# Attention with negated scores: one pass that clips and finds the least, 1/sum by way of HBM, and a new written order

## The chip, the cores and the metric

The kernel runs on one core of one Trainium2 chip. Its time is device time in microseconds (us) of one execution; the figure used is the median of several runs. The engines of a core are TensorE (PE; its weight loads are PEld), VectorE (DVE), ScalarE (ACT), GpSimd (POOL) and SyncE (SP), which here issues every DMA.

## The reference, cut

```python
q_bits = (np.einsum('bhsd,dk->bhsk', q, proj) > 0).astype(np.int64)
k_bits = (np.einsum('bhsd,dk->bhsk', k, proj) > 0).astype(np.int64)
powers = 2 ** np.arange(n_bits)
q_bucket = np.sum(q_bits * powers, axis=-1)
k_bucket = np.sum(k_bits * powers, axis=-1)
mask = q_bucket[:, :, :, None] == k_bucket[:, :, None, :]
scores = scale * np.matmul(q, k.transpose(0, 1, 3, 2))
scores = np.where(mask, scores, -1000000000.0)
scores = scores - np.max(scores, axis=-1, keepdims=True)
attn = np.exp(scores)
attn = attn / (np.sum(attn, axis=-1, keepdims=True) + 1e-09)
return np.matmul(attn, v).astype(np.float32)
...
h = x @ w_in
r = np.maximum(h, 0.0)
g = s * (r * r) + b
return (g @ w_out).astype(np.float32)
...
a = x @ w1
b = x @ w2
h = a * b @ w3
return (h @ w_out).astype(np.float32)
```

The first part is attention over 2 batches of 8 heads, 768 rows, head dimension 64, scale 1/8, with a mask from 6 hash bits. Its output, as 1536 tokens of 512, goes through the second part (512 to 2048 and back) and then the third (two projections to 1024, their product, two more matrices). All of it is float32.

## The kernel before

**Tiling.** Attention runs head by head (16 heads), each in 3 units of 256 query rows, and a unit in two halves of 128 rows (`unit`). For a half, four matmuls write one score tile `sc`, 128 x 768, in PSUM: two of q and k, and two that add products of hash bits, by which every differing bit lowers a score by 2^100 (`mask`, with `thr` and `sgn`). Four operand tiles of a head (`q1`, `q2`, `k1`, `k2`) hold high and low parts of q and k and the mask rows; for head 0 engines build them by halves (`begin`), for the others six DMAs of 64 x 768 per head move their rows (`move`, L373, on SP). The score tiles have two buffers, so a third score waits until `exp` has read the first.

**From score to exp.** Four steps per half, 96 halves in all: DVE takes the row's maximum, negated (`negm`, L487); DVE makes `gate`, which is 1/8 where the row has any unmasked score and 0 else (L495); DVE makes `bias` = negm x gate (L502); ACT computes `p` = exp(sc x gate + bias) and the row's sum `ssum` (L510).

**From exp to output.** PE transposes `p` in 128 x 128 blocks into `t` (L524, 12 to a unit, four to a PSUM tile). Each `t` is split in a high and a low part: two of three by ACT and DVE (L562, L566), the third by ACT and POOL (L545, L550 or L552, L556). PE multiplies them with v into `o` (L530, L531). ACT and DVE add the halves of `o` into `xf` (L579, L583), where two heads stand together.

**1/sum** (`norm`, once for each pair of heads and unit, 24 times): DVE takes the reciprocal of four sums per row (`r`, L604), POOL spreads it to 128 x 256 (`rb`, L610), PE transposes it in two blocks into a PSUM tile `rt` (L620), and DVE multiplies `xf` with it (L624). Then `xf` becomes high and low parts of x (`put_x`).

**The rest.** The second part (`layer1`) multiplies weights with x, three matmuls per product of high and low parts (`h`, `x` at L705); its batch 0 runs between the attention of batch 1. The third part (`layer2`) follows (`psw`, `p`, `y`). Weights come as float64 halves and are taken apart on DVE, ACT and POOL (`convert`, L255 to L269) during attention, are kept in HBM and fetched again.

**Order.** Nothing is scheduled at run time. `Plan` collects the operations; `ORDER` is a table that gives the order in which they are emitted, `WAYS` picks an engine where an operation has several, and `PLACES` gives each tile its buffer. Each engine and the one DMA queue of SP work their instructions off in that order, each waiting for its semaphores. 24 matmuls on a tile of ones (`warm`, L308) stand in the first 26 us on PE, six ahead of the first real ones, the others between the first scores.

Of the kernel before, what the change touches and what calls it, by code (L numbers as in the profile page):

```python
# [38 lines left out]
NW2 = 14  # L39
POOL = {(b, u, 1) for b in range(2) for u in range(3)}  # L40
# [8 lines left out]
    "CqEgFdDNDgDECrDkDODIEhDFCsEkEiDlDJDBEjElFeCwDpDPDhDGDvEmCxE4EnDqDiEoDKE5EQDmEUDLDwDrE9DnEVE6DMDQE7DjE+E8HFDo"
    "EZE/ERDRHMFha6EaHNHGFAESDsFBHLEbEtCyEpFiDtEWIeHHFfFjNdDuDxFmEuFkEXHIFlETFnHJDSEqEyCzHKHODUGBFoDTHPFpErDyFqEY"  # L50
    "DzEcGCFCEvEdGGEzGDEeEwFGGEE0GFHQEsGHHEFLD0FDaoExDVGIFHGjD1GJFEGKE1FIGkFrF6E2FJFvFMGlGoGmE3GnFNFFIgGpFKFwF0Ga"
    "FsInIhF7HTGqGbGrImF1FtFOGsHUGLFxGPKQFPF2HYaxFgGQHVHWFQIkHXHZG8IfIiFyFuIlIpHsGMHaIjF8HRGUHbHtIqFzHSHcagF3GNIo"
    "GtGRGVHuHxHvF4GWGSHwG2HyGxIFGyF5IrHzH0GOayH1IGF9GzGTGXF+GuIHIKF/IIGYGvG0G3HdGZIJHhG4GwKSILG1HeG5GAKaHiIMHfHm"
    "LsG6GcIuINKTKZG9HnG7KYGdIOIvHgH2HoIzG+H3IwGeKUHjIxH4H/IyHkI0H6IsJOH7I1KVItHlGfI2JPG/I3KWGhHpHAKbIAJHJQKXJTGi"
    "LrHqH8JRIBIYKcJSITH9JUIPHBJwHrIUHCJVJWH5JIKdJxJXGgH+KRICazIQI8IVJyIDJ1IRI9IWJzIEI4IZJ2ISJ0JBLtJ3IXIaI5KgLuL0"
    "J4JCI6LzJ5IbKhL1JcJYIcJDJJKlJdI+KiKjIdLxKkI/KmLvI7KeLyL2K5KfJZKnLwa0JhKoK6L3JnJAKpawJEJeJaaYJ+JiK7JfJ6K8JFL4"
    "JjK+K9O4JGKDa1JbJ/K/Jga2J7LSKJKAJoa3LAKKLBJ8JkLCLTJKKuJlJpLXJLKEKBLUJmKvKqLVKFJMJ9LWLYNfKCKGKrLZNgNmKzLaKHNl"
    "KsL7L5bJKILbJqL8KtJNLDK0L9MAJrL+K1JuL/LHKwMBNhKLLIKxMbNiLELMMCLFNjL6MDMcKMMEKyNoK2NnKNLNMdNkMgLJK3MeMULcLOJs"
# [1151 lines left out]
```

## Time and profile before

| | us |
|---|---|
| median of 3 runs | 761.66 (759.51 to 762.94) |
| profiled execution, own time | 762.2 |
| profiled execution, span | 760.4 |

| engine | busy us | share of the span | instructions |
|---|---|---|---|
| PE | 743.4 | 98% | 4392 |
| DVE | 611.4 | 80% | 1221 |
| ACT | 394.3 | 52% | 763 |
| POOL | 286.1 | 38% | 328 |

The busy time of an engine is the union of its instructions from start to end. Matmuls overlap on PE, so a PE that is busy all the time may still start its matmuls later than it could; what a matmul costs in a dense stretch is the distance between two starts, not its duration. Shares are means over the span: attention with little else fills PE's queue up to about 150 us, attention and the second part together up to about 370 us, then come matrices alone.

### The profile page before, as it was taken

To read this page: it belongs to the slowest core of one execution; us is meant where nothing else is said; L and a number is where in the kernel's file an instruction comes from. 1 tells how busy PE (TensorE), PEld (TensorE's weight loads), DVE (VectorE), ACT (ScalarE), POOL (GpSimd) and SP (SyncE) were. 2 spreads that over 40 slices of the span, in tenths; PEclk is the share of its full clock that TensorE was granted. 3 is DMA by queue.
4 is the path that set the end of the run, shared out by engine and by line. 5 is a ranking of instruction groups with operands and counts; after the bars stand their busy time and mean duration, and the time that the engine had idled before them with its cause. 6 is when DMAs were issued, how large, how long until landed. Compare 5 with 4: busy or idle time off the path is not lost.

```text
span 760.4 us, 12708 instructions
## 1 busy us (share of the span) xinstructions
PE 743.4 (98%) x4392; PEld 700.7 (92%) x4392; DVE 611.4 (80%) x1221; ACT 394.3 (52%) x763; POOL 286.1 (38%) x328
## 2 busy tenths in 40 slices
PE   8899999999999999999999999999999999999998
PEld 6898999899998999999999998999998999899996
DVE  7999999999999999998999676775889966655442
ACT  5888898888656666747454242243443321221002
POOL 2577788884635654535311131123304300001101
PEclk9999999999999999999999999999999999999999
DMA  7556565356267674365697997778899997474712
GB/s 223 156 127 175 166 191 145 103 140 198 73 176 234 203 228 144 94 222 174 242 330 238 306 326 250 240 246 286 288 334 346 332 324 254 153 253 130 230 33 84
DMA packets 73823, 159.63 MB, mean 210 GB/s; under 512 B 7328, under 2 KB 41504, under 8 KB 73760
## 3 DMA queue, kind: packets, MB, share of 16 engines
q1 hardware_dynamic: 73760, 158.82, 65.6%
q8 instruction: 35, 0.57, 0.3%
q14 instruction: 28, 0.23, 0.1%
HBM read 99.94 MB, written 41.16 MB: 186 GB/s over the span
## 4 chain that ended last, share of the span: by engine, by line
PE 81%; DVE 11%; DMA 3%; ACT 2%; issue 1%; POOL 0%; POOLq 0%; ACTq 0%; DVEq 0%; SPq 0%
PE x L705 15%; PE h L705 14%; PE p L705 14%; PE y L1149 9%; PE sc L473 7%; PE t L524 6%; PE psw L1108 5%; PE o L530 3%; PE o L531 3%; DVE negm L487 2%; PE bits L445 2%; DVE pt L566 1%; ACT p L510 1%; DMA raw_wo<-in_wo 1%; DMA raw_w_a<-in_w 1%
## 5 line engine op out<-in xcount | busy, mean ns | idle before, releaser
L705 PE MATMUL h<-x,w_wi 128*128 128x384 f32 x768 | 149.8, 339 | 1.8 <-DVE rl L779 1.4
L705 PE MATMUL x<-g,w_wo 128*128 128x384 f32 x768 | 146.5, 337 | 0.8 <-DMA w_wo<-kept_wo 0.5
L705 PEld LDWEIGHTS h<-x,w_wi 128*128 128x128 f32 x768 | 132.7, 188 | 5.9 <-DVE rl L779 2.5
L705 PEld LDWEIGHTS x<-g,w_wo 128*128 128x128 f32 x768 | 133.4, 188 | 3.3 <-issue 0.8
L510 ACT ACTIVATE p<-sc,bias,gate 128x768 f32<-128x768 f32 x96 | 95.7, 997 | 25.6 <-DVE bias L502 19.8
L1078 DVE TENSOR_TENSOR c<-c,p 128x384 f32<-128x384 f32 x112 | 60.3, 552 | 58.5 <-PE p L705 53.2
L487 DVE TENSOR_REDUCE negm<-sc 128x1 f32<-128x768 f32 x96 | 90.9, 949 | 6.4 <-PE sc L473 5.5
L473 PE MATMUL sc<-k,q 128*128 128x384 f32 x384 | 88.8, 354 | 1.8 <-ACT p L510 1.8
L524 PE MATMUL t<-ident,p 128*128 128x128 f32 x576 | 84.0, 275 | 3.5 <-DVE pt L566 1.3
L530 PE MATMUL o<-pt,vv 128*128 128x256 f32 x288 | 78.5, 299 | 0.3 <-DVE xf L583 0.2
L705 PE MATMUL p<-x,w 128*128 128x384 f32 x384 | 76.5, 336 | 0.6 <-DVE c L1078 0.6
L524 PEld LDWEIGHTS t<-ident,p 128*128 128x128 f32 x576 | 67.6, 141 | 9.0 <-DVE pt L566 2.3
L531 PE MATMUL o<-pt,vv 128*128 128x256 f32 x288 | 73.4, 282 | 0.1
L556 POOL TENSOR_TENSOR pt<-pf,pt 128x512 fp32r<-128x512 f32 x48 | 63.2, 1316 | 26.9 <-ACT pt L552 22.8
L705 PEld LDWEIGHTS p<-x,w 128*128 128x128 f32 x384 | 67.9, 188 | 4.0 <-DVE c L1078 1.2
L473 PEld LDWEIGHTS sc<-k,q 128*128 128x128 f32 x384 | 66.3, 194 | 3.7 <-ACT p L510 3.1
L566 DVE TENSOR_TENSOR pt<-t,pt 128x512 fp32r<-128x512 f32 x96 | 65.1, 681 | 4.2 <-ACT pt L562 3.5
L562 ACT CAST pt<-t 128x512 fp32r<-128x512 f32 x96 | 55.7, 586 | 20.0 <-PE t L524 13.7
L530 PEld LDWEIGHTS o<-pt,vv 128*128 128x128 f32 x288 | 54.3, 189 | 2.6 <-DVE xf L583 1.6
L531 PEld LDWEIGHTS o<-pt,vv 128*128 128x128 f32 x288 | 54.5, 189 | 0.4 <-DVE gate L495 0.3
L784 ACT ACTIVATE g<-rl,b_bc 128x384 fp32r<-128x384 f32 x64 | 39.0, 614 | 24.4 <-DVE rl L779 12.6
L1108 PE MATMUL psw<-w_wo,w_w 128*128 128x512 f32 x192 | 51.3, 394 | 0.0
(257 smaller groups left out, 1291.9 us busy)
## 6 DMA issues: line engine op xcount, KB each, us to landing
w<-kept_s SPq DMA_DIRECT2D x64, 256.0 KB, 5.4
...
```

The costliest lines, as they stand in the source:

```text
L473: nc.tensor.matmul(sc()[:, i, :HALF], x[:, t], y[:, i * HALF : (i + 1) * HALF], start=st, stop=not st)
L487: lambda j=j, sc=sc: nc.vector.tensor_reduce(negm()[:, j : j + 1], sc()[:, :, :HALF], AX.XY, ALU.max, negate=True),
L510: lambda j=j, k=k, sc=sc: nc.scalar.activation(ps[j](), sc()[:, :, :HALF], AF.Exp, bias=bias()[:, j : j + 1], scale=gate()[:, j : j + 1], ...
L524: nc.tensor.transpose(tp()[:, e, j * P : (j + 1) * P], flat[:, c * P : (c + 1) * P], ident)
L530: nc.tensor.matmul(o()[:, :U], w, pt()[:, 0, e], start=(c == 0), stop=False)
L531: nc.tensor.matmul(o()[:, :U], w, pt()[:, 1, e], start=False, stop=(c == NC - 1))
L556: lambda pf=pf, pt=pt: nc.gpsimd.tensor_tensor(pt()[:, 1], pf(), r32(pt()[:, 0]), ALU.subtract),
L566: lambda tp=tp, pt=pt: nc.vector.tensor_tensor(pt()[:, 1], tp(), r32(pt()[:, 0]), ALU.subtract),
L705: nc.tensor.matmul(ps()[:, :n], x, y, start=(i == 0 and e == 0), stop=(i == len(terms) - 1 and e == 2))
L1078: "cadd", "dve", 0.47, rank, lambda: nc.vector.tensor_tensor(x(out), a(), p(), op), [(ps, 1), *reads], writes
L1108: nc.tensor.matmul(ps(), w3()[:, p, c], wo()[:, q], start=(j == 0 and e == 0), stop=(j == 7 and e == 2))
L1149: nc.tensor.matmul(y(), abt()[:, p, c], wt()[:, q], start=(i == 0 and e == 0), stop=(i == DF2 // P - 1 and e == 2))
```

## The change

Scores come out negated. q is multiplied with -1/8 as it is loaded (a new operation of 64 x 768 per head, L380 of the new file; for head 0 the factor `qs` goes into the split), the projection gets a factor that undoes this for the bits, and the signs of the mask are turned, so that a differing bit raises a score by 2^100. One DVE instruction per half then clips the score tile at 10^9, in place in PSUM, and finds the row's least value with its accumulator (`least`, L513). exp takes that as bias and -1 as scale (L521). `gate` and `bias` are gone. A fully masked row is all 10^9 and gives exp(0) everywhere, as the reference asks.

1/sum: DVE writes each reciprocal eight times into 128 x 32 (L617) and transposes that in 32 x 32 blocks (L624); two DMAs write rows of 32 into HBM (`rd`, L630), two DMAs read them back, spread over 64 partitions each (`rb`, L640); DVE or POOL multiplies (L644). `rt` and its two transposes on PE are gone, and the spreading on POOL.

Of the warm-up matmuls 15 remain, in one row ahead of all else (`warm`, L312). The tables `ORDER`, `WAYS` and `PLACES` are new as a whole.

```diff
...
+OUT = 1e9
...
+NWARM = 15
...
-    "AgAAAEAhAaCEAVaZAUCFABAiACAXAjADaRAkAZAoahAnAtAKApAuAlAyAxAGCGAmAvAqAYAwA0CNATAzCMCHAbAsD2AHA1ArCIA2CSaaA+CJ"
+    "XyAkA6XjBpAxXkAsXzAyAoBtXqAtA3A7DMApBuX0DNA4A8AqA5BPBvXlBsX1AuBMEbXmXrArBQAvAzBRDOAwBNA0XnDVBBA1DUByXsA2DPX5"
...
+    qs = const.tile([P, 1], F32, name="qs")
+    nc.vector.memset(qs[:D], -(D**-0.5))
+    nc.vector.memset(qs[D:], 1.0)
...
-    for a, t, f in ((0, 2.0**-126, 1.0), (32, 0.0, -1.0), (64, 0.0, -BIG), (96, 2.0**-126, BIG)):
+    for a, t, f in ((0, 2.0**-126, -1.0), (32, 0.0, 1.0), (64, 0.0, -BIG), (96, 2.0**-126, BIG)):
...
-        plan.op(
-            "neg_p", "dve", 0.1, LATER, lambda: nc.vector.tensor_scalar_mul(pj[:, 32:96], pj[:, 32:96], -1.0),
-            [("pj", 0)], [("pj", 1)],
-        )
+        def signs():
+
+            a, c = pj.rearrange("p (a n) -> p a n", n=D)[:, :, : D // 2], pj[:, :D]
+            nc.vector.tensor_scalar_mul(a, a, -1.0)
+            nc.vector.tensor_scalar_mul(c, c, D**0.5)
+
+        plan.op("neg_p", "dve", 0.2, LATER, signs, [("pj", 0)], [("pj", 1)])
...
-        for i in range(24):
-            tw = plan.tile(ps_o, 1, [P, 512], F32, "o", f"warm_{i}", 2)
-            plan.op(
-                "warm", "pe", 0.12, LATER,
-                lambda tw=tw: nc.tensor.matmul(
-                    tw()[:, :U], ones()[:, 0, 0, :P], ones()[:, 0, 0], start=True, stop=True
-                ),
-                [(ones, 0)], [(tw, 0)],
-            )
+        tw = plan.tile(ps_o, 1, [P, 512], F32, "o", "warm", 2)
+
+        def warm_up():
+            for _ in range(NWARM):
+                nc.tensor.matmul(tw()[:, :U], ones()[:, 0, 0, :P], ones()[:, 0, 0], start=True, stop=True)
+
+        plan.op("warm", "pe", 0.12 * NWARM, LATER, warm_up, [(ones, 0)], [(tw, 0)])
...
-                copy(f"split_h{ph}", (0.73, 0.8), q1, t, [(t, 0)], [(q1, 0)])
-                rest(f"split_l{ph}", 1.8, k2, t, q1, [(t, 0), (q1, 0)], [(k2, 0)])
+                less = lambda eng: eng.tensor_scalar(t()[:D], t()[:D], -(D**-0.5), 1.0, ALU.mult, ALU.mult)
+                plan.op(
+                    f"scale{ph}", "pool", 0.8, LATER, lambda: less(nc.gpsimd), [(t, 0)], [(t, 1)],
+                    (
+                        ("dve", 0.46, lambda: less(nc.vector)),
+                        ("act", 0.85, lambda: nc.scalar.mul(t()[:D], t()[:D], -(D**-0.5))),
+                    ),
+                )
+                copy(f"split_h{ph}", (0.73, 0.8), q1, t, [(t, 1)], [(q1, 0)])
+                rest(f"split_l{ph}", 1.8, k2, t, q1, [(t, 1), (q1, 0)], [(k2, 0)])
...
-                ways(f"split_h_0{i}", lambda c=c: q1()[:, c], lambda c=c: t()[:, c], [(t, i)], [(q1, 0, i)])
+                times = lambda eng, c=c: eng.tensor_scalar(q1()[:, c], t()[:, c], qs, 1.0, ALU.mult, ALU.mult)
+                plan.op(
+                    f"split_h_0{i}", "act", 0.52, -500,
+                    lambda c=c: nc.scalar.activation(q1()[:, c], t()[:, c], AF.Copy, scale=qs), [(t, i)], [(q1, 0, i)],
+                    (("dve", 0.43, lambda f=times: f(nc.vector)), ("pool", 0.75, lambda f=times: f(nc.gpsimd))),
+                )
...
-                    lambda c=c: nc.vector.tensor_tensor(k2()[:, c], t()[:, c], r32(q1()[:, c]), ALU.subtract),
+                    lambda c=c: nc.vector.scalar_tensor_tensor(
+                        k2()[:, c], t()[:, c], qs, r32(q1()[:, c]), ALU.mult, ALU.subtract
+                    ),
...
-            negm, gate, bias = (plan.tile(sm_p, 4, [P, NQ], F32, t, f"{t}_{m}") for t in ("negm", "gate", "bias"))
+            least = plan.tile(sm_p, 4, [P, NQ], F32, "least", f"least_{m}")
...
-                    f"max{j}{ph}", "dve", 0.87, LATER,
-                    lambda j=j, sc=sc: nc.vector.tensor_reduce(
-                        negm()[:, j : j + 1], sc()[:, :, :HALF], AX.XY, ALU.max, negate=True
+                    f"max{j}{ph}", "dve", 1.03, LATER,
+                    lambda j=j, sc=sc: nc.vector.tensor_scalar(
+                        sc()[:, :, :HALF], sc()[:, :, :HALF], OUT, None, ALU.min, ALU.min, accum_out=least()[:, j : j + 1]
...
-                    [(sc, 0)], [(negm, j)],
-                )
-
-                plan.op(
-                    f"gate{j}{ph}", "dve", 0.07, LATER,
-                    lambda j=j: nc.vector.tensor_scalar(
-                        gate()[:, j : j + 1], negm()[:, j : j + 1], BIG / 1024, D**-0.5, ALU.is_lt, ALU.mult
-                    ),
-                    [(negm, j)], [(gate, j)],
-                )
-                plan.op(
-                    f"bias{j}{ph}", "dve", 0.13, LATER,
-                    lambda j=j: nc.vector.tensor_scalar_mul(
-                        bias()[:, j : j + 1], negm()[:, j : j + 1], gate()[:, j : j + 1]
-                    ),
-                    [(gate, j)], [(bias, j)],
+                    [(sc, 0)], [(sc, 1), (least, j)],
...
-                        ps[j](), sc()[:, :, :HALF], AF.Exp, bias=bias()[:, j : j + 1], scale=gate()[:, j : j + 1],
+                        ps[j](), sc()[:, :, :HALF], AF.Exp, bias=least()[:, j : j + 1], scale=-1.0,
...
-                    [(sc, 0), (gate, j), (bias, j)], [(ps[j], 0), (ssum, (h % 2, k))],
+                    [(sc, 1), (least, j)], [(ps[j], 0), (ssum, (h % 2, k))],
...
-            plan.op(
-                f"r{b}", "dve", 0.08, at_, lambda: nc.vector.reciprocal(r()[:, :, c], ssum()[:, :, c]),
-                [(ssum, ("e", u))], [(r, u)],
-            )
-            rb = plan.tile(sm_p, 1, [P, NQ, 2, D], F32, "rb", f"rb_{m}")
-            plan.op(
-                f"rb{b}", "pool", 0.35, at_,
-                lambda: nc.gpsimd.tensor_scalar(
-                    rb(), r()[:, :, c].rearrange("p a k -> p k a").to_broadcast([P, NQ, 2, D]),
-                    1.0, 1.0, ALU.mult, ALU.mult,
+            r = plan.tile(sm_p, 1, [P, 32], F32, "r", f"r_{m}")
+            plan.op(
+                f"r{b}", "dve", 0.255, at_,
+                lambda: nc.vector.reciprocal(
+                    r().rearrange("p (k a e) -> p a k e", a=2, k=NQ),
+                    ssum()[:, :, c].unsqueeze(3).to_broadcast([P, 2, NQ, 16 // NQ]),
...
-                [(r, u)], [(rb, 0)],
-            )
-            rt = plan.tile(ps_t, 3, [P, 512], F32, "t", f"rt_{m}")
-
-            def turn_r():
-                for j in range(NQ):
-                    nc.tensor.transpose(rt()[:, j * P : (j + 1) * P], rb()[:, j].rearrange("p a d -> p (a d)"), ident)
-
-            plan.op(f"turn_r{b}", "pe", 0.22, at_ + 0.05, turn_r, [(rb, 0)], [(rt, 0)])
-            plan.op(
-                f"norm{b}", "dve", 0.34, at_ + 0.1, lambda: nc.vector.tensor_tensor(xf(), rt()[:, :U], xf(), ALU.mult),
-                [(rt, 0), (xf, 0), (xf, 1)], [(xf, 2)],
+                [(ssum, ("e", u))], [(r, 0)],
+            )
+            rq = plan.tile(sm_p, 1, [P, 32], F32, "rq", f"rq_{m}")
+            plan.op(f"flip{b}", "dve", 0.125, at_, lambda: nc.vector.transpose(rq(), r()), [(r, 0)], [(rq, 0)])
+            rd = dram.tile([2, U], F32, tag=f"rd_{m}", name=f"rd_{m}", bufs=1)
+
+            def gather_r():
+
+                for a in range(2):
+                    nc.sync.dma_start(
+                        rd[a].rearrange("(t i) -> t i", i=32),
+                        rq().rearrange("(t a e) i -> a t e i", a=2, e=16 // NQ)[a, :, 0],
+                    )
+
+            plan.op(f"rw{b}", "dma", 0.92, at_, gather_r, [(rq, 0)], [("rd", m)])
+            rb = plan.tile(sm_p, 3, [P, U], F32, "tmp", f"rb_{m}")
+
+            def spread():
+                for a in range(2):
+                    nc.sync.dma_start(rb()[a * D : (a + 1) * D], rd[a : a + 1].to_broadcast([D, U]))
+
+            plan.op(f"rr{b}", "dma", 0.92, at_ + 0.02, spread, [("rd", m), (xf, 1)], [(rb, 0)])
+            turned = lambda t: t().rearrange("p (k n i) -> p n k i", k=NQ, i=32)
+            mul = lambda eng: eng.tensor_tensor(
+                turned(xf), rb().rearrange("p (n k i) -> p n k i", k=NQ, i=32), turned(xf), ALU.mult
+            )
+            plan.op(
+                f"norm{b}", "dve", 0.34, at_ + 0.1, lambda: mul(nc.vector), [(rb, 0), (xf, 0), (xf, 1)], [(xf, 2)],
+                (("pool", 0.72, lambda: mul(nc.gpsimd)),),
...
```

What the tables make of it, at three places. Names carry their numbers: `sc_1_0` is unit 1, half 0; `bits_0_1` is head 0, half 1; a last number is the instance's.

PE in the first stretch, where scores of head 0 stand ahead of the first transposes; before:

```order
L308 MATMUL warm_23_347<-ones_205 128x256
L308 MATMUL warm_9_350<-ones_205 128x256
L473 MATMUL sc_0_0_355<-k1_0_235,q1_0_226 128x384 x2
L473 MATMUL sc_0_0_355<-k2_0_231,q2_0_243 128x384 x2
L308 MATMUL warm_3_362<-ones_205 128x256
L308 MATMUL warm_13_368<-ones_205 128x256
L308 MATMUL warm_4_373<-ones_205 128x256
L308 MATMUL warm_0_375<-ones_205 128x256
L473 MATMUL sc_1_0_388<-k1_0_235,q1_0_226 128x384 x2
L473 MATMUL sc_1_0_388<-k2_0_231,q2_0_243 128x384 x2
L524 MATMUL t_0_1_394<-ident_61,p_0_0_385 128x128
```

and now:

```order
L462 MATMUL bits_1_0_306<-k2_1_299,pj_h_86 128x384
L499 MATMUL sc_0_1_313<-k1_0_266,q1_0_259 128x384 x2
L499 MATMUL sc_0_1_313<-k2_0_271,q2_0_279 128x384 x2
L499 MATMUL sc_0_0_323<-k1_0_266,q1_0_259 128x384 x2
L499 MATMUL sc_0_0_323<-k2_0_271,q2_0_279 128x384 x2
L462 MATMUL bits_1_1_333<-q1_1_291,pj_h_86 128x384
L462 MATMUL bits_1_1_333<-q1_1_291,pj_l_87 128x384
L462 MATMUL bits_1_1_333<-k2_1_299,pj_h_86 128x384
L499 MATMUL sc_1_1_345<-k1_0_266,q1_0_259 128x384 x2
L499 MATMUL sc_1_1_345<-k2_0_271,q2_0_279 128x384 x2
L535 MATMUL t_0_2_352<-ident_61,p_0_0_343 128x128
```

Before, five score tiles, with fillers among them, stand ahead of the first transpose; now there are three, the first two of them the two halves of unit 0.

DVE around the scores of unit 4; before:

```order
L487 TENSOR_REDUCE negm_4_552<-sc_4_0_535 128x1
L583 TENSOR_TENSOR xf_0_567<-o_0_479,tmp_0_533 64x256
L495 TENSOR_SCALAR gate_4_571<-negm_4_552 128x1
L258 TENSOR_SCALAR raw_wi_0_0_3_452<-raw_wi_0_0_3_452 128x512
L502 TENSOR_SCALAR bias_4_579<-negm_4_552,gate_4_571 128x1
L487 TENSOR_REDUCE negm_4_552<-sc_4_1_561 128x1
L566 TENSOR_TENSOR pt_1_2_569<-t_1_2_525,pt_1_2_569 128x512
L495 TENSOR_SCALAR gate_4_571<-negm_4_552 128x1
L259 SCALAR_TENSOR_TENSOR raw_wi_0_0_3_452<-raw_wi_0_0_3_452 128x512
L502 TENSOR_SCALAR bias_4_579<-negm_4_552,gate_4_571 128x1
```

and now:

```order
L513 TENSOR_SCALAR sc_4_0_522,least_4_532<-sc_4_0_522 128x2x384
L577 TENSOR_TENSOR pt_1_2_520<-t_1_2_502,pt_1_2_520 128x512
L513 TENSOR_SCALAR sc_4_1_542,least_4_532<-sc_4_1_542 128x2x384
L617 RECIPROCAL r_3_573<-ssum_0_340 128x2x2x8
L259 TENSOR_SCALAR raw_wi_0_0_3_460<-raw_wi_0_0_3_460 128x512
L577 TENSOR_TENSOR pt_2_2_565<-t_2_2_550,pt_2_2_565 128x512
L260 SCALAR_TENSOR_TENSOR raw_wi_0_0_3_460<-raw_wi_0_0_3_460 128x512
L513 TENSOR_SCALAR sc_5_0_583,least_5_604<-sc_5_0_583 128x2x384
L594 TENSOR_TENSOR xf_1_615<-o_1_534,tmp_1_581 64x256
```

Each half had three instructions with others between them, and now has one; a reciprocal of 1/sum stands two rows later.

SP around the last moves of head 7, where 1/sum of units 15 to 17 (heads 4 and 5) comes by; before:

```order
L373 DMA k1_7_1673<-q1_7_1656 64x768 x2
L373 DMA q2_7_1688<-q1_7_1656 64x768
L373 DMA q1_7_1656<-k2_7_1671 64x768
L373 DMA q2_7_1688<-mm_7_1740 64x768
L683 DMA kept_wi_0_0_3_129<-w_wi_0_0_3_699 128x1024
L683 DMA kept_wi_0_0_0_126<-w_wi_0_0_0_408 128x1024
L373 DMA k2_7_1671<-mm_7_1740 64x768
L339 DMA t_9_1807<-in_qkT 128x768
L373 DMA k1_8_1912<-q1_8_1897 64x768 x2
```

and now:

```order
L375 DMA q2_7_1607<-mm_7_1654 64x768
L375 DMA q1_7_1571<-k2_7_1599 64x768
L640 DMA rb_15_1722<-rd_15_135 64x256 x2
L630 DMA rd_16_136<-rq_16_1730 8x32 x2
L375 DMA k2_7_1599<-mm_7_1654 64x768
L640 DMA rb_16_1791<-rd_16_136 64x256 x2
L630 DMA rd_17_137<-rq_17_1811 8x32 x2
L375 DMA k1_8_1838<-q1_8_1809 64x768 x2
L341 DMA t_10_1860<-in_qkT 128x768
```

Among the moves of heads 7 and 8 there are now writes (`rd`) and reads (`rb`) of 1/sum; the read of unit 16 waits in the queue for the write two rows ahead of it, and what stands behind waits with it.

## Rows read from the trace of the kernel before

**Rows 1.** Table by stretches: us, then each engine's busy us, PEclk, DMA share, GB/s

```profile
0.00:40.00 40.00, 34.98 (x163) 28.94 (x164) 33.16 (x80) 28.36 (x53) 14.97 (x21) 0.96 0.64 181
40.00:280.00 240.00, 234.65 (x1615) 223.86 (x1614) 227.37 (x493) 189.26 (x377) 163.78 (x194) 1.00 0.58 163
280.00:742.00 462.00, 459.10 (x2555) 436.09 (x2554) 346.44 (x642) 172.64 (x327) 105.30 (x111) 1.00 0.72 242
742.00:760.40 18.40, 14.65 (x65) 11.81 (x64) 4.46 (x8) 4.02 (x8) 2.05 (x2) 1.00 0.22 86
```

**Rows 2.** Chain of work, dense pieces of PE: start us, us, what

```profile
94.38 1.31 PE t L524 x12
...
373.48 16.12 PE x L705 x93
```

**Rows 3.** Timeline, PE, two products: start us, us, engine, line, operation

```profile
54.78 0.28 PE L530 MATMUL o<-pt,vv 128*128 128x256 f32 x1
54.90 0.28 PE L531 MATMUL o<-pt,vv 128*128 128x256 f32 x1
```

**Rows 4.** Groups of instructions on PE, 40 to 280 us: busy us, mean ns, idle before

```profile
L473 PE MATMUL sc<-k,q 128*128 128x384 f32 x288 | 65.0, 348 | 0.2 <-ACT p L510 0.2
L524 PE MATMUL t<-ident,p 128*128 128x128 f32 x436 | 63.2, 274 | 2.7 <-DVE pt L566 1.3 <-DVE rl L779 0.9 <-DVE acc L799 0.5
L530 PE MATMUL o<-pt,vv 128*128 128x256 f32 x220 | 60.1, 300 | 0.3 <-DVE xf L583 0.2
L531 PE MATMUL o<-pt,vv 128*128 128x256 f32 x221 | 56.3, 282 | 0.0
L705 PE MATMUL h<-x,w_wi 128*128 128x384 f32 x192 | 39.2, 341 | 0.4 <-ACT pf L545 0.4
L705 PE MATMUL x<-g,w_wo 128*128 128x384 f32 x150 | 30.1, 340 | 0.0
L445 PE MATMUL bits<-q,pj_h 128*128 128x384 f32 x24 | 9.0, 374 | 0.1
...
L620 PE MATMUL rt<-ident,rb 128*128 128x128 f32 x36 | 7.1, 278 | 1.6 <-DVE pt L566 1.5
```

**Rows 5.** Timeline, first 23 us: start us, us, engine, line, operation, idle before

```profile
12.02 0.96 DVE L487 TENSOR_REDUCE negm<-sc 128x1 f32<-128x768 f32 x1 [0.54 <-PE sc L473]
...
13.78 0.20 DVE L502 TENSOR_SCALAR bias<-negm,gate 128x1 f32<-128x1 f32 x1
14.09 0.99 ACT L510 ACTIVATE p<-sc,bias,gate 128x768 f32<-128x768 f32 x1 [3.53 <-DVE bias L502]
...
20.61 0.98 ACT L510 ACTIVATE p<-sc,bias,gate 128x768 f32<-128x768 f32 x1
...
22.12 1.06 PE L524 MATMUL t<-ident,p 128*128 128x128 f32 x4
```

**Rows 6.** Groups of instructions on DVE, whole span, from the page

```profile
L487 DVE TENSOR_REDUCE negm<-sc 128x1 f32<-128x768 f32 x96 | 90.9, 949 | 6.4 <-PE sc L473 5.5
...
L502 DVE TENSOR_SCALAR bias<-negm,gate 128x1 f32<-128x1 f32 x96 | 19.8, 206 | 1.5
...
L495 DVE TENSOR_SCALAR gate<-negm 128x1 f32<-128x1 f32 x96 | 13.8, 146 | 1.2
```

**Rows 7.** DMA issues: tiles, count, KB each, median us from issue to landing

```profile
k<-mm SPq DMA_DIRECT2D x15, 192.0 KB, 3.2
...
s_bc<-in_sv SPq DMA_DIRECT2D x1, 0.5 KB, 4.6
```

**Rows 8.** Timeline, last move of head 3 and its first score

```profile
50.10 0.46 SPq L373 DMA_DIRECT2D k<-mm  x1
...
55.85 0.94 PE L473 MATMUL sc<-k,q 128*128 128x384 f32 x4
```

**Rows 9.** Table by stretches, 21.0 to 24.2 us: the granted clock is PEclk

```profile
21.00:24.20 3.20, 3.20 (x12) 3.07 (x12) 2.46 (x5) 2.15 (x5) 2.96 (x3) 0.50 0.00 0
```

More of the change, by code (lines that the diff above doesn't have):

```diff
@@ L39 @@
 NW2 = 14
+NWARM = 15
+FILLS = ()
 POOL = {(b, u, 1) for b in range(2) for u in range(3)}
@@ L49 @@
[L49 to L58, printed above, removed]
@@ L405, in ways @@
                 plan.op(
-                    key, "act", 0.4, -500, lambda: nc.scalar.copy(out(), in_()), reads, writes,
+                    key, "act", 0.52, -500, lambda: nc.scalar.copy(out(), in_()), reads, writes,
                     (
-                        ("dve", 0.27, lambda: nc.vector.tensor_copy(out(), in_())),
+                        ("dve", 0.38, lambda: nc.vector.tensor_copy(out(), in_())),
                         ("pool", 0.75, lambda: nc.gpsimd.tensor_scalar(out(), in_(), 1.0, 1.0, ALU.mult, ALU.mult)),
@@ L448, in mask, with fill @@
             at_ = -500 if need else LATER
-            plan.op(f"bits{key}", "pe", 0.525, at_, project, [*(need or [(q1, 0), (k2, 0)]), ("pj", 3)], [(bits, 0), ("bits", n, i)])
+            plan.op(f"bits{key}", "pe", 0.525, at_, project, [*(need or [(q1, 0), (k2, 0)]), ("pj", 3), *([(tw, 0)] if need and i == 0 else [])], [(bits, 0), ("bits", n, i)])
+            if n == 0 and i == 0:
+                for e, count in enumerate(FILLS):
+                    def fill(count=count):
+                        for _ in range(count):
+                            nc.tensor.matmul(tw()[:, :HALF], pj_h, q1()[:, c], start=True, stop=True)
+                    plan.op(
+                        f"warm{e + 1}", "pe", 0.165 * count, LATER, fill, [("bits", 0, 0), (q1, 0, 0), ("pj", 3), (tw, e)],
+                        [(tw, e + 1)],
+                    )
             plan.op(
@@ L460, in unit @@
             q1, q2, k1, k2, vv = ops[n]
-            negm, gate, bias = (plan.tile(sm_p, 4, [P, NQ], F32, t, f"{t}_{m}") for t in ("negm", "gate", "bias"))
+            least = plan.tile(sm_p, 4, [P, NQ], F32, "least", f"least_{m}")
             if h % 2 == 0 and u == 0:
-                sums[n] = sums[n + 1] = tuple(
-                    plan.tile(sm_p, 2, [P, 2, NU * NQ], F32, t, f"{t}_{n}") for t in ("ssum", "r")
-                )
-            ssum, r = sums[n]
+                sums[n] = sums[n + 1] = plan.tile(sm_p, 2, [P, 2, NU * NQ], F32, "ssum", f"ssum_{n}")
+            ssum = sums[n]
             ps = [plan.tile(p_p, 5, [P, 2, HALF], F32, "p", f"p_{m}_{j}") for j in range(NQ)]
@@ L576, in unit @@
             xf = xfs[u]
-            tmp = plan.tile(sm_p, 2, [P, U], F32, "tmp", f"tmp_{m}")
+            tmp = plan.tile(sm_p, 3, [P, U], F32, "tmp", f"tmp_{m}")
             plan.op(
@@ L586, in unit @@
             if h % 2 == 1:
-                norm(m, u, xf, ssum, r)
+                norm(m, u, xf, ssum)
                 t0 = b * S + u * U
@@ L590, in unit, with norm @@
                     put_x(m, g, h // 2, xf, t0)
-        def norm(m, u, xf, ssum, r):
+        def norm(m, u, xf, ssum):
             b = heads[units[m][0]][0]
```

177 lines of the change are left out of this document (91 added, 86 removed).

## The prediction, made before the changed kernel ran

> **What bounds the kernel now.** First the table by stretches [rows 1]: PE is busy 234.65 of the 240 us from 40 to 280 us and 459.10 of the 462 us after that. So the time is PE's, and an edit counts if it takes matmuls off PE, lets PE start its real work earlier, or closes gaps between matmuls. DVE is busy 227.37 of the 240, so it is nearly as full there, and falls to 346.44 of 462 behind; ACT has 189.26 of 240.
>
> "Busy" hides gaps, since matmuls overlap. So the second view is the distance between starts in dense pieces: 16.12 us for 93 matmuls of 384 columns is 0.1733 each, 1.31 for 12 transposes 0.109 [rows 2], and two products of 256 columns stand 0.12 apart [rows 3]. With the counts from 40 to 280 us [rows 4] (`bits` has three groups of 24, of which one is shown): 288 + 192 + 150 + 72 = 702 by 0.1733 is 121.7; 436 + 36 = 472 by 0.109 is 51.5; 220 + 221 = 441 by 0.12 is 52.9. That is 226.1 of 240: **13.9 us** are gaps, most of them too short for the list of waits.
>
> The third view is the first 22 us [rows 5]. The first score tile is ready for DVE at 12.02, its exp starts at 14.09, yet the first transpose starts at 22.12: it needs both halves of unit 0, and the exp of the second starts only at 20.61. In between PE does five scores and fillers.
>
> **The change, part by part.**
>
> *1/sum off PE.* 24 pairs of transposes go (36 of the 48 instructions lie in this stretch [rows 4]): 48 by 0.109 = **5.2 us**, all on the path, since PE is full where they stand. In their place DVE gets a longer reciprocal and a transpose, 24 each, and SP 96 small DMAs. No PE instruction waits on these directly, but x does; the cover is that x is wanted a head pair or more later. What it costs if the cover is gone is a rival below.
>
> *gate and bias off DVE, clip for maximum.* The three cost 949 + 146 + 206 ns = 1.301 us of DVE per half [rows 6]. No row shows DVE writing to PSUM. The nearest is the maximum itself, which reads the same tile, 0.949; that is the low end. The high end is a clip that reads and then writes, one after the other, 2 x 0.949 = 1.90. I take 1.05, because that row has the same elements and source, and an accumulator's result should cost at most about one of the small instructions (0.146) more; so 1.05 lies between 0.95 and 1.10. Here a page bears on it: the Trainium skill, "VectorE: DVE Perf Modes", section "Two Vector instructions with no wait between them", treats an operation that writes its accumulator as two instructions, the main one and a read. No row here shows that on DVE. By that rule the clip would be 0.949 + 0.146 = 1.10, and the gain below would be about 1 us less, 747.7 in place of 746.7.
>
> From 40 to 280 us there are 288 / 4 = 72 halves. DVE loses 72 x 0.352 = 25.3 us and gains 72 x 0.10 = 7.2, and for 18 pairs of reciprocal and transpose at most 18 x 0.206 = 3.7 net. So 227.4 becomes about 213, and DVE's slack grows from 12.6 to about 27 us. The wait from score to exp also gets shorter by the two steps and what stands between them. How much of the 13.9 us of gaps goes can't be read off. It is at least 0; 10 is the high end, since ACT and the buffers stay. I take **5.0**, about a third: 1.6 of it is the wait that stands ahead of `rt` itself [rows 4], which goes with `rt`, and the rest is waits behind DVE.
>
> *Start.* On PE the two halves of unit 0 now come first. The path to the first score holds the same work; a scaling by DVE ahead of head 0's mask makes it longer and a later `pj` load may, and the missing fillers make it shorter, so I leave the first pass over a score at 12.0. Clip to 13.05, exp at 13.1, a microsecond earlier than now. The second score stands right behind the first, so its clip runs about 13.35 to 14.4 and its exp starts at 14.45, where now it starts at 20.61: 6.2 earlier. The transposes follow it by 1.5 as now (22.12 - 20.61), at about 16. By then PE has done two scores fewer, 8 x 0.1733 = 1.4. Net **4.8 us**. From 2.5 (first pass 2 us later) to 6.2 (the two scores find room in later gaps).
>
> *The rest.* Scaling q adds 15 instructions, 8 on POOL, 5 on DVE, 2 on ACT, by the order; multiplying xf goes to POOL in 18 of 24 cases. POOL has 163.78 of 240 [rows 1], so that is hidden; if POOL were late, x would be, not the scores. After 280 us the work is the same and the written order much the same, so I count nothing, give or take 2.
>
> **Sum.** 5.2 + 5.0 + 4.8 = 15.0. The span of 760.4 becomes 745.4, the profiled execution's 762.2 becomes 747.2, and since that lies 0.5 above the median of the runs, the forecast is **746.7 us**.
>
> **The rivals.**
>
> *More goes.* 10 us of gaps and 6.2 at the start: 5.2 + 10 + 6.2 = 21.4, about 740. For it speaks that the whole order was written anew for a lighter DVE; against it, ACT is as busy as before.
>
> *ACT takes DVE's place.* exp, two splits and the copies stay on ACT, and a few of POOL's splits move to it. Then of the gaps only the 1.6 at `rt` go: 761.7 - 5.2 - 4.8 - 1.6 = 750.1. Against it: 189.26 of 240 [rows 1].
>
> *The low clock at the start.* From 21.0 to 24.2 us the granted clock is 0.50, that is 1.2 of 2.4 GHz [rows 9], after a stretch in which PE stood between fillers and waits. The fillers between the scores are gone now, so PE has longer idle pieces before and between them. If the low level lasts from 16 us until PE is dense, the work there counts twice: 12 transposes 1.3, three scores 2.1, 12 products 1.4, together 4.8 more, 751.5. The Trainium skill, "TensorE: Matmul & The Clock Gate", part 1, has the same direction: the array starts throttled, activity releases it, and idleness brings the throttle back. By that rule dropping the fillers speaks against this change; the row agrees in that the low level came back once after waits.
>
> *The gains are given back.* If x of batch 0 can't be ready earlier, whatever the start wins is lost at the first product of the second part: only 5.2 stays, 756.5. That is also how the change would fail to do what it says: PE's freed slots would turn into waits.
>
> *SP held by the way through HBM.* A read of 1/sum waits in SP's queue for its write to land, and the moves of the next head's operands stand behind it. Now the last move of a head (`k<-mm`) is issued at 50.10, lands in 3.2 [rows 7], and the head's first score starts at 55.85 [rows 8]: slack 2.55. The one tiny DMA on record took 4.6 to land among large ones [rows 7], 2.05 over the slack. If that meets a third of the 24, 8 x 2.05 = 16.4 eat the gain: 763.1. Against it: most reads stand three or more rows behind their writes.
>
> *Slower: the clip in place.* At 1.90 a half costs DVE 0.6 more than now; 72 x 0.6 = 43.1, less the slack of 12.6, is 30.5 on the path, as DVE is then fuller than PE. With 5.2 from `rt` and 3.1 at the start: 761.7 + 30.5 - 8.3 = 783.9. It decides from where (clip - 1.301) x 72 exceeds 12.6 + 8.3, at 1.59. For it: no row shows the form. Against it: reading PSUM goes at the rate of the other operations.
>
> **How the numbers follow.** A measurement of this kernel can tell about 0.5% from no change, so faster means below 757.9 and slower above 765.5. Chances: forecast (743 to 750) 0.40; more goes (738 to 743) 0.14; ACT 0.16; low clock 0.08; given back 0.08; SP held 0.08; clip 0.06. The range from 738 to 757 holds the first five but for a part of "given back" and the low edge of "more goes": about 0.82. Faster is the first four and most of the fifth, 0.85; the same is the rest of it and most of "SP held", 0.07; slower is the clip and the tail of "SP held", 0.08.
>
> **What would show it.** In the profile after: no `rt` and PE's gaps from 40 to 280 us, counted as above, near 9 in place of 13.9 less `rt`; DVE busy near 213 in that stretch; a clip between 0.95 and 1.10; the first transpose near 16 us; the granted clock in the first 25 us. Wrong would be: a first transpose after 19; a clip over 1.3; SP waiting on `rd` with PE's scores waiting for moves; gaps after 280 us over 2 us more than now.

## The result, and the profile after

The changed kernel took **743.45 us** (median of 4 runs, 742.94 to 744.77), the kernel before 762.3 on the same chip: ratio 0.9759, 95% interval 0.9725 to 0.9792, 18.8 us less by the spans of the profiled executions (760.4 and 741.6). The forecast was 746.7 with a range from 738 to 757.

The table by stretches of the changed kernel, to lay beside [rows 1]; columns as there:

```profile
0.00:40.00 40.00, 32.73 (x171) 28.81 (x172) 32.73 (x77) 30.82 (x61) 19.07 (x24) 0.96 0.71 206
40.00:280.00 240.00, 238.47 (x1648) 231.57 (x1647) 225.81 (x447) 190.71 (x392) 171.57 (x200) 1.00 0.63 179
280.00:742.00 462.00, 457.41 (x2520) 433.96 (x2518) 336.92 (x610) 173.67 (x332) 95.34 (x97) 1.00 0.71 242
```

Its groups on PE from 40 to 280 us, to lay beside [rows 4]; `rt` is gone:

```profile
L499 PE MATMUL sc<-k,q 128*128 128x384 f32 x298 | 67.0, 346 | 0.0
L535 PE MATMUL t<-ident,p 128*128 128x128 f32 x440 | 64.6, 273 | 0.3 <-DVE pt L577 0.2
L541 PE MATMUL o<-pt,vv 128*128 128x256 f32 x224 | 60.7, 298 | 0.8 <-POOL x L663 0.7
L542 PE MATMUL o<-pt,vv 128*128 128x256 f32 x224 | 57.0, 282 | 0.0
L729 PE MATMUL h<-x,w_wi 128*128 128x384 f32 x192 | 38.8, 340 | 0.0
L729 PE MATMUL x<-g,w_wo 128*128 128x384 f32 x192 | 38.4, 341 | 0.4 <-DVE acc L823 0.4
L462 PE MATMUL bits<-q,pj_h 128*128 128x384 f32 x26 | 9.4, 362 | 0.1
```

Counted as before: 298 + 192 + 192 + 3 x 26 = 760 by 0.1733 is 131.7; 440 by 0.109 is 48.0; 448 by 0.12 is 53.8; together 233.5. So 6.5 us are gaps where 13.9 were, and PE does more in the same stretch (`x` 192 in place of 150).

The start, to lay beside [rows 5] (start us, us, engine, line, operation, idle before):

```profile
5.68 0.19 DVE L296 TENSOR_SCALAR pj<-pj 128x64 f32<-128x64 f32 x1 [3.91 <-DMA pj<-in_projp]
...
8.12 0.87 DVE L380 TENSOR_SCALAR t<-t 64x768 f32<-64x768 f32 x1
...
13.09 0.97 DVE L513 TENSOR_SCALAR_CACHE_REDUCE sc<-sc 128x768 f32<-128x768 f32 x1 [0.50 <-PE sc L499]
...
13.97 0.14 DVE L513 DVE_READ_ACCUMULATOR sc<-sc 128x1 f32 x1
...
14.14 0.90 ACT L521 ACTIVATE p<-sc,least 128x768 f32<-128x768 f32 x1 [0.79 <-DVE sc L513]
...
15.42 0.90 ACT L521 ACTIVATE p<-sc,least 128x768 f32<-128x768 f32 x1 [0.29 <-DVE sc L513]
...
16.47 1.59 PE L535 MATMUL t<-ident,p 128*128 128x128 f32 x12 [0.31 <-ACT p L521]
```

The first transpose starts at 16.47, where it started at 22.12; the first pass over a score starts 1.07 later than it did. By counts from 0 to 40 us (the groups of PE without fillers) PE has done 70 matmuls of 384 columns, 52 transposes and 34 products of 256 columns, 21.9 us of work, and 66, 45 and 28 before, 19.7: it is 2.2 us ahead at 40 us. A second profiled execution of the changed kernel, further below, has 23.0 by the same count, so this lead varies by about 1 us from one execution to the next.

The pass over a row and its exp, to lay beside [rows 6] (groups over the whole span: busy us, mean ns, idle before):

```profile
L513 DVE TENSOR_SCALAR_CACHE_REDUCE sc<-sc 128x768 f32<-128x768 f32 x96 | 91.8, 957 | 5.3 <-PE sc L499 4.3
...
L521 ACT ACTIVATE p<-sc,least 128x768 f32<-128x768 f32 x96 | 87.0, 907 | 10.9 <-PE t L535 5.5 <-DVE sc L513 4.6
...
L513 DVE DVE_READ_ACCUMULATOR sc<-sc 128x1 f32 x96 | 12.9, 134 | 0.2
```

A clip takes 957 ns and its accumulator is read by a second DVE instruction of 134 ns; 13.09 to 14.11 is 1.02 us from first start to last end. exp takes 907 ns, and it took 997 before.

**Where the 18.8 us went:** `rt` 5.2, gaps from 40 to 280 us 13.9 - 6.5 = 7.4, start 2.2, and what is left, 4.0, after 280 us. That last figure is a difference of the others: counting the work that is left after 280 us in the same way gives 5.0, so it is good to about 1 us. The waits listed there for `x`, `h` and `p` add up to 3.0 us before and 0.4 after.

### The profile page after: what moved, and what is told of

Its sections match the earlier page's. It is cut to its first block, busy times and chain, and to the rows that moved or that the text cites. A ratio compares the mean times of both kernels' runs of the same rounds, so it can differ in the third digit from the quotient of the medians.

```text
span 741.6 us, 12689 instructions
## 1 busy us (share of the span) xinstructions
PE 728.6 (98%) x4335; PEld 694.3 (94%) x4335; DVE 595.5 (80%) x1132; ACT 395.2 (53%) x783; POOL 286.0 (39%) x319
## 4 chain that ended last, share of the span: by engine, by line
PE 62%; DVE 2%; ACT 0%; issue 0%; DVEq 0%
PE p L729 16%; PE x L729 15%; PE h L729 13%; PE y L1173 9%; PE psw L1132 6%; PE t L535 1%; PE sc L499 1%; PE o L541 1%; PE o L542 1%; DVE c L1102 0%; DVE pt L577 0%; DVE raw_w_a L259 0%; DVE raw_wi L260 0%; ACT pt L573 0%; PE bits L462 0%
## 5 line engine op out<-in xcount | busy, mean ns | idle before, releaser
L729 PE MATMUL h<-x,w_wi 128*128 128x384 f32 x768 | 147.7, 338 | 0.1
L513 DVE TENSOR_SCALAR_CACHE_REDUCE sc<-sc 128x768 f32<-128x768 f32 x96 | 91.8, 957 | 5.3 <-PE sc L499 4.3
L521 ACT ACTIVATE p<-sc,least 128x768 f32<-128x768 f32 x96 | 87.0, 907 | 10.9 <-PE t L535 5.5
L798 ACT ACTIVATE rl<-h 128x384 f32<-128x384 f32 x64 | 31.5, 492 | 47.9 <-PE h L729 39.3
L541 PEld LDWEIGHTS o<-pt,vv 128*128 128x128 f32 x288 | 55.1, 191 | 1.9 <-POOL x L663 0.9
L542 PEld LDWEIGHTS o<-pt,vv 128*128 128x128 f32 x288 | 55.2, 192 | 0.3
```

The source lines that it names most:

```text
L513: lambda j=j, sc=sc: nc.vector.tensor_scalar(sc()[:, :, :HALF], sc()[:, :, :HALF], OUT, None, ALU.min, ALU.min, accum_out=least()[:, j : j ...
L521: lambda j=j, k=k, sc=sc: nc.scalar.activation(ps[j](), sc()[:, :, :HALF], AF.Exp, bias=least()[:, j : j + 1], scale=-1.0, accum_out=ssum( ...
L541: nc.tensor.matmul(o()[:, :U], w, pt()[:, 0, e], start=(c == 0), stop=False)
L542: nc.tensor.matmul(o()[:, :U], w, pt()[:, 1, e], start=False, stop=(c == NC - 1))
L729: nc.tensor.matmul(ps()[:, :n], x, y, start=(i == 0 and e == 0), stop=(i == len(terms) - 1 and e == 2))
```

## The experiments

**Parts alone, in the old order.** The first kernel is the one before with the score part (signs, clip, no gate and bias, exp with a constant scale); the scaling of q stands with the split. The second has 1/sum by way of HBM, with the writes where POOL spread 1/sum and the reads where PE turned it; one read, which would have had to wait for a buffer in use, stands a few rows later. The third has both.

```
 scores_old
-    nc.vector.tensor_reduce(negm[:, j], sc[:, :, :HALF], AX.XY, ALU.max, negate=True)
-    gate = ...; bias = ...
+    nc.vector.tensor_scalar(sc, sc, OUT, None, ALU.min, ALU.min, accum_out=negm[:, j])
-    activation(ps[j], sc, AF.Exp, bias=bias[:, j], scale=gate[:, j], accum_out=...)
+    activation(ps[j], sc, AF.Exp, bias=negm[:, j], scale=-1.0, accum_out=...)
+    nc.gpsimd.tensor_scalar(t[:D], t[:D], -(D**-0.5), 1.0, ALU.mult, ALU.mult)   # ahead of split_h
 hbm_old
-    plan.op(f"rb{b}", "pool", ...)      # spread 1/sum
+    plan.op(f"rb{b}", "dma", ..., gather_r)   # two writes of rd
-    plan.op(f"turn_r{b}", "pe", ...)    # two transposes
+    plan.op(f"turn_r{b}", "dma", ..., spread) # two reads into rb
 both_old: both edits
```

> The score part alone in the old written order: negated scores, clip with the least in one pass, no gate and bias, exp with the least as bias and the constant -1 as scale; the scaling of q stands on POOL just ahead of the split. 1/sum stays on PE, and so does the old order of the start. Theory (a lighter DVE closes gaps by itself): DVE from 40 to 280 us falls by about 18 us, PE's gaps there fall by 3 to 5 us, the end comes at 756 to 759 us. Rival (the new order brings it): the old order has DVE work standing where gate and bias stood, PE waits for the same transfers and conversions as before, 760 to 763 us.

> 1/sum by way of HBM alone in the old written order: the writes stand in SP's queue where POOL spread 1/sum before, the reads where PE turned it. Theory (48 transposes at 0.109 go from a full PE): 5.2 us less, 757 us, DVE's multiplication waits at times for a read. Rival (SP held): the reads stand a few rows behind their writes in the old order, so SP waits for the landing, the moves of the next head come later and PE's scores wait: 761 to 770 us.

> Both parts, in the old written order. Theory (the parts carry most of it): the sum of the two runs before it, 751 to 755 us, and the rest to 743.5 us is the new order, about 8 to 11 us. Rival (the order carries it): 758 us or more, so that the new order alone is worth 14 us or more.

Measured: 758.59 (ratio 0.996, 0.9946 to 0.9974), **831.06** (1.093, 1.0906 to 1.0955) and 830.84 (1.093, 1.0889 to 1.0971). The score part alone brings 3 us, as its theory had it, though DVE is 9.6 us less busy from 40 to 280 us (217.81) where 18 were expected. Its gaps in that stretch, counted as above (730, 468 and 432), are 10.6, in a profiled execution of 755.49 that was the fastest of twelve. The way through HBM alone costs 69.5 us. No expectation had that size. Its rival named the cause, a read close behind its write, but not who waits. This is the third kernel; first its multiplication by 1/sum (a group on DVE), then what PE waited for from 40 to 280 us (us, times, longest), then the timeline of one case:

```profile
L649 DVE TENSOR_TENSOR xf<-rb,xf 128x256 f32<-128x256 f32 x24 | 14.1, 587 | 54.5 <-DMA rb<-rd 54.2
```

```profile
PE t L552 <- DVE pt L594: 18.2, 6, 5.6
PE o L558 <- DVE xf L611: 9.3, 5, 4.4
PE bits L477 <- DVE pt L594: 4.6, 3, 4.2
```

```profile
96.42 1.24 SPq L639 DMA_DIRECT2D rd<-pj  x2
...
99.03 1.10 SPq L646 DMA_DIRECT2D rb<-rd  x2
...
102.17 0.42 DVE L649 TENSOR_TENSOR xf<-rb,xf 128x256 f32<-128x256 f32 x1 [3.05 <-DMA rb<-rd]
102.52 0.68 DVE L594 TENSOR_TENSOR pt<-t,pt 128x512 fp32r<-128x512 f32 x1
...
103.26 0.62 PE L552 MATMUL t<-ident,p 128*128 128x128 f32 x2 [2.78 <-DVE pt L594]
```

The write goes out at 96.42, the read at 99.03, and the multiplication at 102.17 has kept DVE idle for 3.05 us. Behind it in DVE's queue stands the remainder `pt` (102.52), and for that PE has waited 2.78. In all, DVE idles 54.2 us for these reads; PE's scores, for which the forecast feared, hardly wait (idle 0.1 ahead of `sc` from 40 to 280 us). The granted clock is lower too in this stretch, in which PE idles: 0.92 in the mean (third number from the end), where the kernel before has 1.00. How much of the loss is the clock's, no run tells.

```profile
40.00:280.00 240.00, 200.64 (x1301) 191.03 (x1300) 181.58 (x364) 153.00 (x317) 139.04 (x158) 0.92 0.49 134
```


**The multiplication later.** The same with each multiplication, and the conversions of x behind it, 30 rows later where their consumers leave room.

```
+    moved[norm], moved[xh], moved[xl] = min(row + 30, first consumer - 1)
```

> As the run with both parts in the old order, but each multiplication by 1/sum and the two conversions of x behind it stand 30 rows later in the written order (some 6 us), where their consumers leave room; writes and reads of 1/sum stay where they are in SP's queue, but for the few that wait for the buffer. In the run before, 16 multiplications made DVE wait 54.2 us for the read. Theory (DVE waits in its own queue, and that is the loss): these 54 us go, the time falls from 830.8 to 755 to 785 us. Rival (SP held: the reads wait in SP's queue and the transfers behind them come late): it stays above 805 us, with PE waiting for moves of operands.

Measured: 790.81 (1.038, 1.0348 to 1.0412). 40 of the 70 us are back, so the theory holds for the larger part, though its range (755 to 785) was missed. Of the rest, the waits and SP's timeline show one piece:

```profile
L672 DVE TENSOR_TENSOR xf<-rb,xf 128x256 f32<-128x256 f32 x24 | 16.6, 692 | 11.5 <-DMA rb<-rd 11.3
```

```profile
PE o L581 <- DVE xf L634: 14.8, 13, 4.4
```

```profile
217.29 1.24 SPq L662 DMA_DIRECT2D rd<-pj  x2
...
240.09 0.33 SPq L730 DMA_DIRECT2D raw_wo<-in_w_out  x1
...
250.84 1.72 SPq L669 DMA_DIRECT2D rb<-rd  x2
```

```profile
SPq L730 <- POOL w_wi L302: 9.4, 2, 8.6
```

DVE's idle time is down to 11.5, but PE's products wait 14.8 us for `xf` (L634), the addition that has to read `o` first; for 5.8 us of that stretch DVE in turn waits there for POOL's conversion of x, which stands later now and still holds the buffer. The read behind the write of 217.29 leaves SP at 250.84: between them stand loads of weights, for whose buffers SP waits (9.4 us for POOL alone, last row: us, times, longest). SP is held here, in one place of 24, but the other way about than the rival had it: the loads hold up the read, and not the read what stands behind it. How the remaining 30 us divide was not settled. In the changed kernel the new order keeps writes, reads and multiplications apart (73.62, 78.99 and 82.75 us for a unit of heads 2 and 3), and 18 of 24 multiplications stand on POOL, which idles 8.5 us for them; DVE idles for none. Whether the distance or the change of engine does more was not tested: no run has these multiplications on POOL in the old order.

**exp with a tile for its scale.**

```
-    bias=least[:, j], scale=-1.0
+    bias=least[:, j], scale=minus      # 128x1, holds -1
```

> The changed kernel, but exp takes its scale -1 from a 128x1 tile and not as a constant. In the changed kernel exp takes 907 ns in the mean, before 997 ns. Theory (the constant makes exp shorter, and ACT has slack): exp is back near 1.0 us, ACT is busy 8.6 us more over 96 exps, and the time is 743 to 745 us. Rival 1 (part of the gaps closed because of the shorter exp): 746 us or more. Rival 2 (exp is shorter for another reason, such as less traffic in PSUM): exp stays at 0.90 to 0.92 us.

Measured: 743.44 (0.9755, 0.973 to 0.978).

```profile
L523 ACT ACTIVATE p<-sc,least,minus 128x768 f32<-128x768 f32 x96 | 95.9, 1000 | 10.6 <-PE t L537 5.5 <-DVE sc L515 4.3
```

exp is back at 1000 ns, and the time is the same: the theory. The shorter exp plays no part in the gain.

**DVE's load and the wait, put back.** Two small operations behind each clip: first on constants, then on the least, with exp waiting for the second.

```
 dve_load
+    nc.vector.tensor_scalar(g, qs, BIG, 1.0, ALU.is_lt, ALU.mult)
+    nc.vector.tensor_scalar_mul(h2, qs, g)
 dve_chain
+    nc.vector.tensor_scalar(g, least[:, j], BIG, 1.0, ALU.is_lt, ALU.mult)
+    nc.vector.tensor_scalar_mul(h2, least[:, j], g)
-    exp(..., bias=least[:, j])
+    exp(..., bias=h2)
```

> The changed kernel with two small DVE operations on 128x1 constants behind each clip, which nothing waits for: the time of gate and bias is back on DVE (96 x about 0.35 us = 34 us), but not the wait from score to exp by way of them, except through DVE's own queue. Theory (DVE's load from 40 to 280 us made the gaps): 5 to 8 us come back, 748 to 752 us. Rival (the gaps closed by the new order, DVE has slack for this): 743 to 746 us.

> The same two operations, but now on the least of the clip and with exp waiting for the second: load and wait as gate and bias had them. If load alone counts, this is the same as the run before within 1 us; if the wait from score to exp counts, it is 2 us or more slower than that run, and the difference is the price of the longer chain.

Measured: 757.24 (0.9948, 0.9928 to 0.9967) and 766.53 (1.0073, 1.0051 to 1.0094). The two operations in the first (groups on DVE), and the row of 40 to 280 us of each:

```profile
L517 DVE TENSOR_SCALAR pj<-qs,pj 128x1 f32<-128x1 f32 x96 | 20.6, 215 | 4.6
...
L516 DVE TENSOR_SCALAR pj<-qs 128x1 f32<-128x1 f32 x96 | 14.2, 148 | 0.3
```

```profile
40.00:280.00 240.00, 233.53 (x1583) 221.02 (x1582) 230.08 (x568) 185.96 (x381) 166.49 (x194) 1.00 0.60 170
```

```profile
40.00:280.00 240.00, 228.19 (x1527) 212.88 (x1527) 230.12 (x553) 182.84 (x373) 164.60 (x192) 1.00 0.59 165
```

0.36 us of load on DVE per half cost 13.8 us, where 5 to 8 were expected, and the wait another 9.3. Gaps by the same count: 6.5 in the changed kernel, 17.0 with the load (708 matmuls of 384 columns, 432 transposes, 443 products of 256), 25.4 with load and wait (675, 420, 432). The last is more than the 13.9 of the kernel before, which has both: the new order is no better for a DVE with the old load; it suits these durations.

**The start.** `pj` first, head 1's scaling, split and bits behind unit 0's scores (rows of the written order), and, apart from it, ten products that nothing reads where PE waits at 18.8 us; then both.

```
 start_anew
-    load_qk_0, load_qk_0, ones, load_p, ... scale0, bits_01, mask_00, split_h0, ... bits00, ... score1s, mask00, score0s
+    load_qk_0, load_p, load_qk_0, ones, ... bits_01, mask_00, ... scale0, split_h0, ... score1s, score0s, ... bits00, ... mask00
 fills
+    if m == 1 and j == 0:
+        for _ in range(10):
+            nc.tensor.matmul(tw()[:, :U], pj_h, q1()[:, :U], start=True, stop=True)
```

> The changed kernel as it is, for the comparison with the three beside it: 743 to 744 us.

> The changed kernel with another written order for the start alone: the load of pj ahead of the second half of head 0, and the scaling, the split and the bits of head 1 behind the scores of unit 0 and not ahead of its masks. In the changed kernel the first clip starts at 13.1 us, where 12.0 was forecast, since DVE waits 3.91 us for pj and then does 0.87 us of head 1 first. Theory (these two made the start term too large): the first clip starts at 10.5 to 11.5 us and the end comes 1 to 2.5 us earlier than in the changed kernel, 741 to 742.5 us. Rival (the start is bound by all of DVE's and ACT's work up to 40 us, not by this chain): no change, 743 to 744 us.

> The changed kernel with 10 products of 256 columns that nothing reads, on PE behind the second unit's second score (from 18.8 us), where PE waits 1.64 us for an exp. In the changed kernel the granted clock is 0.5 from 21.4 to 24.8 us, and 12 products stand 0.21 apart there where 0.12 is usual. Theory (the wait brings the low level): no low level from 21 to 25 us, the end 1 to 1.7 us earlier, 741.8 to 742.8 us. Rival (the low level costs nothing because DVE and ACT are behind anyway): low level gone, time the same, 743 to 744.5 us.

> Both of these together. If both act on PE's path, their gains add: 739.5 to 741.5 us. If they cover each other or lie beside the path: as the better of the two alone.

Measured: 742.42 (0.9743, 0.972 to 0.9766), 743.5 (0.9758, 0.9735 to 0.9781), 743.1 (0.9758, 0.9733 to 0.9783) and 743.12 (0.976, 0.9735 to 0.9784). All the same: both rivals, and none beats the changed kernel. First clip and first transpose of the new start (its timeline) and its row of 13 to 17 us (granted clock is the third number from the end), then 21 to 25 us for the changed kernel, for its second profiled execution and for the fillers:

```profile
11.81 0.95 DVE L513 TENSOR_SCALAR_CACHE_REDUCE sc<-sc 128x768 f32<-128x768 f32 x1
...
15.34 2.17 PE L535 MATMUL t<-ident,p 128*128 128x128 f32 x12
```

```profile
13.00:17.00 4.00, 3.10 (x13) 3.01 (x14) 4.00 (x9) 3.01 (x6) 1.11 (x1) 0.57 0.51 145
```

```profile
21.00:25.00 4.00, 4.00 (x19) 3.70 (x17) 3.90 (x8) 2.32 (x6) 3.18 (x3) 0.57 0.27 93
```

```profile
21.00:25.00 4.00, 3.26 (x23) 2.79 (x21) 3.68 (x9) 2.56 (x6) 3.79 (x3) 1.00 0.50 134
```

```profile
21.00:25.00 4.00, 2.42 (x14) 1.91 (x13) 4.00 (x7) 1.67 (x4) 3.35 (x3) 1.00 0.44 125
```

The first clip is 1.28 us earlier, and nothing of it reaches the end. In this execution the low level of the clock comes at 13 to 17 us, and the twelve transposes take 2.17 us and not 1.59, which eats part of the head start; at 40 us PE has done 23.0 us of work, just as in the changed kernel's second execution (75, 52 and 36 in both). How full the engines are behind the start is seen in these stretches of the changed kernel, PE first, DVE third, ACT fourth:

```profile
15.00:25.00 10.00, 7.90 (x41) 6.85 (x40) 9.90 (x20) 7.65 (x17) 4.01 (x4) 0.83 0.51 138
25.00:40.00 15.00, 14.14 (x99) 12.93 (x98) 14.00 (x29) 13.96 (x29) 10.83 (x11) 1.00 0.79 218
```

DVE is busy 9.90 of 10 and then 14.00 of 15 us (14.73 in the second execution), ACT 13.96 of 15. PE's own waits from 15 to 40 us, 2.9 us, all end on ACT, 2.3 of them on an exp, and the exps wait 2.4 us there for a clip. So from 15 us on PE is paced by the chain through DVE and ACT, with DVE the fullest; this is read from the shares and waits, and no run lightens DVE there alone. The low level of the clock (0.57 in the mean of these 4 us, so mostly 1.2 of 2.4 GHz; PE had waited 1.64 us before) is there in one execution of the changed kernel and absent (1.00) in another, with the same time. With the fillers it is absent and the time is the same too; but as it can be absent without them, that run does not show that they lift it.

**The transposes, put back as bare time.**

```
+    if h % 2 == 1 and j == 0:
+        for i in range(2):
+            nc.tensor.transpose(sc()[:, i, HALF:], ident, ident)
```

> The changed kernel with the 48 transposes back on PE as bare time: two transposes of a constant ahead of the first score of each unit of an odd head, into columns that nothing reads, with no wait of their own. Theory (PE is the path, so their 48 x 0.109 = 5.2 us count in full): 747.5 to 749 us. Rival (PE has gaps of 6.5 us from 40 to 280 us in which DVE is what it waits for, and the transposes fill these): 743.5 to 746 us.

Measured: 747.17 (0.9814, 0.9793 to 0.9834). Against the two ratios of the changed kernel, 0.9759 and 0.9743, that is 4.2 to 5.4 us, each good to 2 or 3 us by the intervals. The time lies just under the theory's 747.5 to 749 and above the rival's 743.5 to 746: most of the transposes' time counts, and little of it fills gaps.

```profile
L498 PE MATMUL sc<-ident 128*128 128x128 f32 x36 | 6.9, 272 | 0.0
```

With 36 of them in the stretch the gaps, by the same count, are 5.9, against 6.5 without.

## Why the prediction was right, and where its terms were not

The time lay in the range, 3 us below the forecast, for reasons that partly cancel: the start brought 2.6 less than its term, the gaps 2.4 more, and that these two come out even is luck. What remains, 4.0 by difference, stands after 280 us, where the forecast counted nothing. Point by point:

- *1/sum off PE, 5.2 us:* right within the interval, as the last experiment shows. Its cover, that x is wanted much later, holds in the new order alone. The rival "SP held" had the right place, but a price (16.4 us) far too low and the wrong victim: in the old order 1/sum through HBM costs 69.5 us, mostly in DVE's queue behind the waiting multiplication. The prediction asked of every added wait what SP holds behind it, and not what DVE does.
- *The clip, 1.05 us:* right; 957 ns and a read of 134 ns, 1.02 from start to end. The slower rival (1.90) is out. The rule of the Trainium skill ("VectorE: DVE Perf Modes", "Two Vector instructions with no wait between them"), that an operation with an accumulator is two instructions, is what the trace shows; their busy times add up to 1.09, but they overlap, so that the sum by that rule (1.10) was a little high.
- *Gaps from 40 to 280 us, 5.0:* mechanism right, size off: 7.4. The step that failed is "about a third". Put back one after the other, DVE's load opens 10.5 us of gaps and the wait 8.4 more. So both matter in the new order; but the two together are more than the 7.4 that closed, so they don't say how those divide. Nor can it be read off the old order: there the same part closes 13.9 - 10.6 = 3.3 us of gaps. DVE was to fall to 213 and is at 225.81: the forecast held the work in the stretch fixed, while the new order moves work from later into it (75 clips where 73 maxima stood, and more weights taken apart). It also priced the longer reciprocal and the transpose at 3.7 us more, where they take 10.4 in place of 3.2, and left out 2.9 of scaling q on DVE.
- *The start, 4.8:* too large by more than half, 2.2. The milestones were near (first transpose 16.47 for 16), the step from them to the end was wrong: it took the earlier transposes for earlier work from then on, though DVE and ACT are nearly full from 15 us. That `pj` and head 1 came first, and so the first clip at 13.09 in place of 12.0, is not the reason, as far as the experiment on the start shows it (its low level lies elsewhere). Nor is the 2.2 shown to be the new order's: with the score part in the old order PE has done 22.0 us of work at 40 us (69, 52 and 36), as much as here, in an execution without the low level.
- *After 280 us, 0 +-2:* 4.0 by difference, outside its bounds. The waits of `x`, `h` and `p` that went are 2.6 of it. That the new order does this is only argued; no run isolates it.
- *The low clock, 751.5:* the level came, its price of 4.8 us didn't: it lasted from 21 to 25 us only, where PE is paced by DVE and ACT. The rule of the Trainium skill that spoke against dropping the fillers ("TensorE: Matmul & The Clock Gate", part 1: activity releases the throttle, idleness brings it back) agrees with the level's coming; the time doesn't follow it here. The kernel before is not as indifferent to the low level: of its 49 executions timed beside the experiments the ten with a mean granted clock of 0.999 or more take 759.5 us in the mean, the other 39 take 761.7; for the changed kernel and the four variants that measured the same it is 742.9 (8) and 743.3 (23). So up to 2 us of the gain may be a start that no longer pays for the low level, an estimate from these means; no trace shows where the level lay in those executions.
